# A gated linear recurrence with a maxout feed-forward block: which units run beside which group of matmuls

## The chip, the cores and the metric

The kernel runs on one core of a Trainium2 chip. The metric is the device time of one execution in microseconds. The core has five engines with instruction streams of their own: TensorE (PE: matmuls, and weight loads, shown as PEld), VectorE (DVE), ScalarE (ACT), GpSimd (POOL) and SyncE (SP, which here only issues DMA transfers). They wait for each other by semaphores. Matmul results go to PSUM, which has banks of 512 float32 values per partition.

## The reference

Two blocks in a row. The first is a recurrence over time for every batch b and head h, with a state matrix of 48 x 48:

```
f = sigmoid(f_logit)                                   # q, k, v, f_logit: (4, 8, 768, 48)
state = f[t][:, None] * state + outer(k[t], v[t])
y[t] = q[t] @ state
```

The second takes y as x with 3072 tokens of 8*48 = 384 features:

```
h = max(x @ w1, x @ w2, x @ w3)                        # w1, w2, w3: 384 x 768
out = h @ w_out                                        # w_out: 768 x 384
```

q, k, v and f_logit are float32. The weights arrive as float64, and the kernel rounds them to float32 itself, word by word.

## The kernel before, in words

**Units and groups.** A chunk is 64 time steps. A unit `u` is one chunk of two batches: 128 tokens with all 8 heads. There are NU = 24 units; even and odd ones belong to two pairs of batches, each with its own running state. Four units (GRP) make 512 tokens, a group for the feed-forward part (FFN); there are six groups, 0 to 5.

**The steps of a unit.** `sigmoids(u)` makes the gates on ScalarE; `scan(u)` makes the products of the gates from behind on VectorE (line 287); `after(u)` multiplies k by them (`kh`, line 298), `before(u)` runs a second scan (line 305) and multiplies q (`qh`, line 309). `keys(u)` turns kh around by four TensorE transposes (line 325) and a ScalarE copy (line 327), or `keys_by_blocks` does the same by 16 transposes of 32 x 32 blocks on VectorE (line 340). `pairs(u)` makes key-query products on TensorE (line 350) and masks them on VectorE (`at`, line 353). `values(u)` multiplies them by v (line 364), makes the new part of the state (line 373) and adds it to the old (`st`, line 381, VectorE); `carry(u)` is the state's decay on GpSimd (line 315). `finish(u)` adds the old state's part to y (line 394) and copies y to `heads` (line 400, ScalarE). The tile `y` has two PSUM banks: columns 0 to 255 of each hold outputs, 256 to 447 the new part of the state. `pack` moves heads into `xT`, the FFN's input, by ten DMA transfers (line 416), since 48 features don't line up with 128 partitions.

**Rows and blocks.** For units below BY_ROWS = 8, f, k and q arrive with tokens on partitions, one transfer a tensor and unit (line 171), and TensorE turns them (line 249). For the others two units arrive together, eight transfers a tensor (line 180), in blocks that VectorE turns (line 254), and the products are GpSimd's.

**The FFN as a generator.** `ffn(g, xT)` is a Python generator. One step makes 128 of the 768 hidden features (j) with one of the three matrices (i): three matmuls (line 443) into one PSUM tile `p`, of which there are two, each a bank. For i = 0 ScalarE copies it to `top` (line 448); for i = 1 and 2 VectorE takes the maximum with it (line 450). float32 matmuls run as two passes, so the trace has two records for each. A step of 512 tokens yields twice, a half-step of 256 tokens once. In group 0 the first two j run by halves, so that the work can start when two units are packed: 12 half-steps. Four output steps follow (matmuls line 469, copy line 472, DMA line 476), with two yields each. Every group has 44 yields.

**The order.** `tc.manual_schedule` takes the order written in the program, on each engine and in each queue. `fill(n)` runs n yields of the oldest FFN generator that is pending. So the numbers of yields say how much FFN work lies on TensorE between the steps of the units. Units 0 to 3 are written out; their gaps on TensorE hold some unused matmuls (`busy`). Then a loop over u = 4 to 23 runs unit u, prepares unit u + 1, and calls fill in between.

**Weights.** `load_weights` fetches them in 24 pieces of 384 KB, nine on GpSimd's queue in the written-out part, the rest on SP's from inside group 0. Each piece is rounded in three parts: `round_begin` (two ScalarE passes, lines 218 and 221), `round_middle` (VectorE's maximum, line 230, and its shift and mask, line 231; GpSimd's addition, line 233) and `round_end` (VectorE, line 240, into `w_in` or `w_out`). Group 0's steps call them ahead of the piece that they need.

Of the kernel before, what the change touches and what calls it, by code (L numbers as in the profile page):

```python
# [11 lines left out]
U32 = mybir.dt.uint32  # L12
# [41 lines left out]
def kernel(  # L54
# [32 lines left out]
    def fast():  # L87
        ctx = ExitStack()
        with ctx:
# [58 lines left out]
            BY_ROWS = 8  # L148
# [65 lines left out]
            def round_begin(n):  # L214
                if n in raw:
                    lo, hi = words(n)
                    top = work.tile([128, PIECE], U32, name="top_bits", bufs=4)
                    nc.scalar.activation(top.bitcast(FP32), hi.bitcast(FP32), AF.Abs)

                    rest = work.tile([128, PIECE], U32, name="rest_bits", bufs=3)  # L220
                    nc.scalar.activation(rest, lo, AF.Copy, scale=2.0 ** -29)
                    halfway[n] = (top, rest)

            def round_middle(n):
                if n in raw:
                    top, rest = halfway[n]

                    nc.vector.tensor_scalar(top.bitcast(FP32), top.bitcast(FP32), HI_MIN, None, op0=ALU.max)  # L230
                    nc.vector.tensor_scalar(top, top, 3, 0x3FFFFFF8, op0=ALU.logical_shift_left, op1=ALU.bitwise_and)  # L231

                    nc.gpsimd.tensor_tensor(top, top, rest, op=ALU.add)  # L233

            def round_end(n):
                if n in raw:
                    (top, _), (_, hi) = halfway.pop(n), words(n)
                    dst = pieces[n][0].bitcast(U32)
                    by = lambda t: t.rearrange("p (a c) -> p a c", a=dst.shape[1])
                    nc.vector.scalar_tensor_tensor(dst, by(hi), 0xC0000000, by(top),  # L240
                                                   op0=ALU.bitwise_and, op1=ALU.bitwise_or)
                    raw.pop(n)
# [76 lines left out]
            def keys(u):  # L319

                if u < min(BY_ROWS, NU - 2):
                    kh = ready[u]["kh"]
                    tr_s = ps_tr.tile([UT, HP, 128], FP32, name="tr")
                    for hp in range(HP):
                        nc.tensor.transpose(tr_s[:, hp, :], kh[:, hp].rearrange("p a t -> p (a t)"), ident)  # L325
                    ks = work.tile([UT, H, DP], FP32, name="ks")
                    nc.scalar.copy(ks.rearrange("s h d -> s (h d)"), tr_s.rearrange("s a d -> s (a d)"))
                    ready[u]["ks"] = ks

            def keys_by_blocks(u, n):  # L330

                if BY_ROWS <= u < NU - 2:
                    kh = ready[u]["kh"]
                    if n == 0:
                        ready[u]["ks"] = work.tile([UT, H, DP], FP32, name="ks")
                    ks = ready[u]["ks"].rearrange("s (hp par) d -> s hp par d", par=2)
                    a, t0 = divmod(n * 32, C)
                    for p0 in range(0, 128, 32):
                        par, e0 = divmod(p0, DP)
                        nc.vector.transpose(ks[n * 32:(n + 1) * 32, :, par, e0:e0 + 32], kh[p0:p0 + 32, :, a, t0:t0 + 32])  # L340
# [82 lines left out]

            def ffn(g, xT):
# [3 lines left out]
                steps = [(j, slice(0, TOK)) for j in range(NJ)]  # L428
                if g == 0:
                    steps = [(j, slice(n * HALF, (n + 1) * HALF)) for n in range(2) for j in range(J_HALF)] + steps[J_HALF:]  # L430
                done, n_step = 2, 0
                for j, t in steps:
                    w = t.stop - t.start
                    for i in range(3):
                        p = ps_f.tile([128, TOK], FP32, name="p")[:, 0:w]
                        for kt in range(NK):
                            if g:
                                rhs = xT[:, kt, :]
                            elif w < TOK:
                                rhs = by_halves(xT)[:, t.start // HALF, kt, :]  # L440
                            else:
                                rhs = by_halves(xT)[:, :, kt, :]
                            nc.tensor.matmul(p if g or w < TOK else p.rearrange("p (two t) -> p two t", two=2),  # L443
# [22 lines left out]
                for i in range(GRP):  # L466
                    p = ps_f.tile([128, TOK], FP32, name="p")
                    for j in range(NJ):
                        nc.tensor.matmul(p[:, 0:DM], lhsT=hm[:, j, i * UT:(i + 1) * UT], rhs=w_out[:, j, :],  # L469
                                         start=(j == 0), stop=(j == NJ - 1))  # L470
                    o = work.tile([UT, DM], FP32, name="o", bufs=3)
                    nc.scalar.copy(o, p[:, 0:DM])  # L472
                    c, bp = divmod(g * GRP + i, 2)
                    for a in range(2):
                        t0 = (2 * bp + a) * S + c * C
                        nc.sync.dma_start(out=out[t0:t0 + C, :], in_=o[a * C:(a + 1) * C, :])
                    yield
                    yield
# [24 lines left out]
            with tc.manual_schedule():  # L503
# [26 lines left out]
                load_weights(3, queue=nc.gpsimd)  # L530
# [9 lines left out]
                after(3)  # L540
                pairs(2)
                finish(1)
                carry(3)
                load_weights(3, queue=nc.gpsimd)
# [4 lines left out]
                for n in range(2):  # L549
                    round_begin(n)  # L550
                values(2)
                keys(3)
                finish(2)
                round_middle(0)
                load_weights(1, queue=nc.gpsimd)
                pairs(3)
# [3 lines left out]
                load_weights(1, queue=nc.gpsimd)  # L560
# [20 lines left out]
                fill(2)  # L581
# [3 lines left out]
                for u in range(GRP, NU):  # L585
                    n = u + 1
                    fill(0 if u == 2 * GRP else 4 if u % 2 and u > 2 * GRP else 2)
                    keys(u)
                    keys_by_blocks(u, 2)
                    if u > GRP:  # L590
                        finish(u - 1)
                        if u % GRP == 3:
                            pack(0, 2, xT)
                        elif u % GRP == 0:
                            pack(3, 3, xT, both)
                    if u % GRP == 0:
                        if u > GRP:
                            pending.append(ffn(u // GRP - 1, xT))
                        xT = new_xT()
                    pairs(u)  # L600

                    if u + 2 < BY_ROWS:
                        load(u + 2)
                    if BY_ROWS <= u + 3 < NU and u % 2:
                        load(u + 3, one, "fkq" if u % GRP == 1 else "f")
# [5 lines left out]
                    fill(2)  # L611
# [4 lines left out]
                    fill(2)  # L616
                    if BY_ROWS <= u + 2 < NU and u % GRP == 0:
# [4 lines left out]
                    fill(1 if u < 2 * GRP else 2)  # L622
                    if BY_ROWS <= u + 2 < NU and u % GRP == 0:
                        load(u + 2, one, "q")
                    keys_by_blocks(n, 0)
                    if u >= 2 * GRP:
                        fill(2)
# [236 lines left out]
```

## Time and profile before

Three runs: 480.65, 481.89 and 482.61 us, median 481.89.

| | |
|---|---|
| profiled execution | 480.5 us |
| its span, first to last instruction | 478.8 us |
| TensorE busy | 456.6 us, 95% |
| VectorE busy | 282.8 us, 59% |
| GpSimd, ScalarE busy | 113.1 us, 102.4 us |
| first FFN matmul | at 34.56 us |
| group 0's last output matmul ends | at 123.6 us |
| last matmul ends, end of the span | 472.1 us, 478.8 us |
| all FFN matmuls (lines 443 and 469) | 290.0 us and 96.3 us busy |
| TensorE clock granted, mean | 0.992 of full speed |

The span is the time from the first instruction to the last; the metric adds 1.7 us in this execution. Busy time sums an engine's instructions. A row of a timeline gives start, duration, engine, line, operation, output and inputs, and in brackets how long the engine had been idle before it and what released it. TensorE's ends are modelled, so two neighbouring rows can overlap a little.

### The profile page before, as it was taken

The page shows a single profiled execution, that of the slowest core. Times are in us where ns is not written, and L with a number is a line of the kernel's source. Part 1 is how long each engine was busy: PE and PEld are TensorE (multiplying, and loading weights), DVE is VectorE, ACT ScalarE, POOL GpSimd, SP SyncE. Part 2 cuts the span into 40 slices and gives each one's busy share as a digit, 9 for nine tenths or more (in the row PEclk, how much of TensorE's full clock was granted, in tenths as well). Part 3 has the DMA queues.
Part 4 walks back from the last instruction along what each step waited for, and adds up shares of the span by engine and source line. Part 5 has one row for each costly group of instructions (what it writes and reads, how often), then busy time and mean ns, then how long its engine had stood idle before and what let it go on. Part 6 is the DMA issues. An engine that isn't in the chain of part 4 may idle for free.

```text
span 478.8 us, 10137 instructions
## 1 busy us (share of the span) xinstructions
PE 456.6 (95%) x4061; PEld 248.5 (52%) x4061; DVE 282.8 (59%) x565; ACT 102.4 (21%) x217; POOL 113.1 (24%) x133
## 2 busy tenths in 40 slices
PE   5978799899999999999999999999999999999994
PEld 4766655556445446555445555445554445444452
DVE  6949998977487584487684587684585210112100
ACT  2546345422012102012102112112112102000000
POOL 2546553441330230330230330330331200000000
PEclk9989999999999999999999999999999999999998
DMA  9997997614466043673042674042620012100012
GB/s 135 211 212 219 200 329 113 89 40 65 99 95 94 12 79 78 104 89 50 2 79 56 112 89 68 1 78 56 117 34 2 1 49 51 33 1 0 1 28 45
DMA packets 167578, 38.53 MB, mean 80 GB/s; under 512 B 154752, under 2 KB 165888, under 8 KB 167520
## 3 DMA queue, kind: packets, MB, share of 16 engines
q1 hardware_dynamic: 162032, 33.16, 39.9%
q0 software_dynamic: 1008, 3.54, 2.7%
q10 hardware_dynamic: 4480, 1.08, 1.5%
q8 instruction: 34, 0.56, 0.5%
q14 instruction: 24, 0.20, 0.1%
HBM read 28.31 MB, written 4.72 MB: 69 GB/s over the span
## 4 chain that ended last, share of the span: by engine, by line
PE 83%; SPq 8%; DMA 4%; DVE 2%; issue 1%; ACT 1%; POOL 0%; DVEq 0%; ACTq 0%; POOLq 0%
PE p L443 52%; PE p L469 20%; PE y L364 3%; PE y L394 2%; SPq L171 2%; SPq L180 2%; PE y L373 2%; PE a L350 2%; DMA q_ld<-in_q_dram 2%; SPq L161 2%; DMA v_ld<-in_v_dram 2%; SPq L416 1%; PE tr L249 1%; PE tr L325 0%; DMA k_ld<-in_k_dram 0%
## 5 line engine op out<-in xcount | busy, mean ns | idle before, releaser
L443 PE MATMUL p<-xT,w_in 128*128 128x512 f32 (+1 forms) x684 | 290.0, 575 | 2.9 <-DVE w_in L240 1.6
L443 PEld LDWEIGHTS p<-xT,w_in 128*128 128x128 f32 x684 | 126.3, 190 | 137.2 <-issue 125.2
L469 PE MATMUL p<-w_out,hm 128*128 128x384 f32 x288 | 96.3, 489 | 0.0
L450 DVE TENSOR_TENSOR top<-p,top 128x512 f32<-128x512 f32 (+1 forms) x38 | 25.0, 657 | 99.5 <-PE p L443 99.5
L469 PEld LDWEIGHTS p<-w_out,hm 128*128 128x128 f32 x288 | 54.0, 190 | 37.6 <-issue 1.9
L340 DVE STREAM_TRANSPOSE ks<-kh 32x128 f32<-32x128 f32 x224 | 67.7, 302 | 3.6
L448 ACT COPY top<-p 128x512 f32<-128x512 f32 (+1 forms) x38 | 21.4, 563 | 175.6 <-PE p L443 175.6
L297 POOL COPY ends<-r 128x8 f32<-128x8 f32 x24 | 7.5, 310 | 186.8 <-DVE r L287 186.8
L450 DVE TENSOR_TENSOR hm<-p,top 128x512 f32<-128x512 f32 (+1 forms) x38 | 24.8, 652 | 29.5 <-PE p L443 29.4
L298 POOL TENSOR_TENSOR kh<-kt,r 128x512 f32<-128x512 f32 x16 | 31.4, 1962 | 36.5 <-DVE kt L254 26.1
L400 ACT COPY heads<-y 64x256 f32<-64x256 f32 (+1 forms) x72 | 26.6, 369 | 48.1 <-PE y L394 34.5
L233 POOL TENSOR_TENSOR top_bits<-top_bits,rest_bits 128x384 uint32<-128x384 uint32 x24 | 28.1, 1171 | 35.6 <-DVE top_bits L231 33.3
L287 DVE TENSOR_TENSOR_SCAN r<-gate,from_one 128x520 f32<-128x520 f32 x24 | 30.6, 1276 | 5.3 <-issue 2.5
L472 ACT COPY o<-p 128x384 f32<-128x384 f32 x24 | 11.4, 476 | 102.4 <-PE p L469 98.7
L305 DVE TENSOR_TENSOR_SCAN prod<-gate,from_inv 128x520 f32<-128x520 f32 x24 | 30.1, 1256 | 0.0
L364 PEld LDWEIGHTS y<-at,v_ld 64*64 64x64 f32 x768 | 13.6, 134 | 18.3 <-issue 15.4
L353 DVE TENSOR_TENSOR at<-a,mask 128x512 f32<-128x512 f32 x24 | 16.6, 691 | 8.3 <-PE a L350 7.9
L254 DVE STREAM_TRANSPOSE gate<-sig 128x512 f32<-128x512 f32 x16 | 11.3, 705 | 15.3 <-ACT sig L269 15.3
L394 PEld LDWEIGHTS y<-qh,state 48*48 48x48 f32 x704 | 11.8, 123 | 15.2 <-issue 13.3
L364 PE MATMUL y<-at,v_ld 64*64 64x64 f32 x768 | 17.1, 225 | 2.7 <-DMA v_ld<-in_v_dram 2.7
L315 POOL TENSOR_TENSOR state<-st,ends 128x384 f32<-128x384 f32 x22 | 19.4, 881 | 0.1
L309 POOL TENSOR_TENSOR qh<-qt,prod 128x512 f32<-128x512 f32 x16 | 18.8, 1176 | 0.8 <-DVE qt L254 0.8
(68 smaller groups left out, 271.1 us busy)
## 6 DMA issues: line engine op xcount, KB each, us to landing
v_ld<-in_v_dram SPq DMA_DIRECT2D x48, 96.0 KB, 3.1
out_dram<-o SPq DMA_DIRECT2D x48, 96.0 KB, 2.3
raw<-in_moe_w_dram POOLq DMA_DIRECT2D x9, 384.0 KB, 6.3
raw<-in_moe_w_dram SPq DMA_DIRECT2D x9, 384.0 KB, 4.7
raw<-in_moe_w_out_dram SPq DMA_DIRECT2D x6, 384.0 KB, 8.0
xT<-heads SPq DMA_DIRECT2D x30, 72.0 KB, 2.1
f_ld<-in_f_logit_dram SPq DMA_DIRECT2D x32, 64.0 KB, 2.7
k_ld<-in_k_dram SPq DMA_DIRECT2D x32, 64.0 KB, 2.6
```

The source lines that it names most:

```text
L233: nc.gpsimd.tensor_tensor(top, top, rest, op=ALU.add)
L287: nc.vector.tensor_tensor_scan(r[:, 0:LEN][:, ::-1], flat(gate)[:, ::-1], flat(from_one)[:, ::-1], 1.0, op0=ALU.mult, op1=ALU.max)
L298: (nc.vector if u < BY_ROWS else nc.gpsimd).tensor_tensor(kh.rearrange("p h a t -> p a h t"), kt, by_batch(r[:, 1:LEN + 1].rearrange("p (x ...
L305: nc.vector.tensor_tensor_scan(flat(prod), flat(gate_tiles[u % 2]), flat(from_inv[u % 2]), 1.0, op0=ALU.mult, op1=ALU.max)
L340: nc.vector.transpose(ks[n * 32:(n + 1) * 32, :, par, e0:e0 + 32], kh[p0:p0 + 32, :, a, t0:t0 + 32])
L364: nc.tensor.matmul(y[o:o + DP, a, hp * C:(hp + 1) * C], lhsT=v_ld[s, 2 * hp + par, :], rhs=d["at"][s, par, hp, :], start=(hp == 0), stop=F ...
L394: nc.tensor.matmul(y[o:o + D, a, hp * C:(hp + 1) * C], lhsT=st[r, a, hp, :], rhs=d["qh"][r, a, hp, :], start=False, stop=(hp == HP - 1), s ...
L400: nc.scalar.copy(heads[o, :, t0 + a * C:t0 + (a + 1) * C], y[i, a, 0:HP * C].rearrange("p (h t) -> p h t", h=HP))
L443: nc.tensor.matmul(p if g or w < TOK else p.rearrange("p (two t) -> p two t", two=2), lhsT=w_in[i][:, kt, j * 128:(j + 1) * 128], rhs=rhs, ...
L448: nc.scalar.copy(top, p)
L450: nc.vector.tensor_tensor(hm[:, j, t] if i == 2 else top, p, top, op=ALU.max)
L469: nc.tensor.matmul(p[:, 0:DM], lhsT=hm[:, j, i * UT:(i + 1) * UT], rhs=w_out[:, j, :], start=(j == 0), stop=(j == NJ - 1))
```

## The change

It has six parts.

1. BY_ROWS is 6, not 8: units 6 and 7 arrive in blocks. A new number BY_BLOCKS = 12 says where `keys_by_blocks` takes over from `keys`: units 6 to 11 have their inputs in blocks but their keys turned by TensorE.
2. Fills: more yields of group 0 go ahead of and into unit 4; two to each gap in units 5 to 11, one to the last gap of units 10 and 11. From unit 12 on the amounts are those of before.
3. Group 1 runs by halves throughout: 18 half-steps and two output steps for units 4 and 5, then the same for units 6 and 7. It is appended in unit 6, after a pack of units 4 and 5; units 6 and 7 are packed in unit 8. It comes to lie beside units 7 to 12.
4. Two half-steps in a row share one PSUM tile, one bank: columns 0 to 255, then 256 to 511. This holds in group 0 too.
5. Weights: the first six pieces are issued together after the gates of unit 3; the next ones and the first roundings move behind the pairs of unit 3.
6. The maximum of `round_middle` reads one tile (`size`) and writes another (`top_bits`), which is 3 x 128 with gaps, where it worked in place on 384 elements in a row. The later operations see it as 3 x 128.

```diff
-            BY_ROWS = 8
+            BY_ROWS = 6
+            BY_BLOCKS = 12
...
-                    top = work.tile([128, PIECE], U32, name="top_bits", bufs=4)
-                    nc.scalar.activation(top.bitcast(FP32), hi.bitcast(FP32), AF.Abs)
+                    size = work.tile([128, PIECE], FP32, name="size", bufs=2)
+                    nc.scalar.activation(size, hi.bitcast(FP32), AF.Abs)
...
+                    top = work.tile([128, 3, PIECE // 3 + 2], U32, name="top_bits", bufs=2)[:, :, 0:PIECE // 3]
-                    nc.vector.tensor_scalar(top.bitcast(FP32), top.bitcast(FP32), HI_MIN, None, op0=ALU.max)
+                    nc.vector.tensor_scalar(top.bitcast(FP32), size, HI_MIN, None, op0=ALU.max)
                     nc.vector.tensor_scalar(top, top, 3, 0x3FFFFFF8, op0=ALU.logical_shift_left, op1=ALU.bitwise_and)
-                    nc.gpsimd.tensor_tensor(top, top, rest, op=ALU.add)
+                    nc.gpsimd.tensor_tensor(top, top, rest.rearrange("p (a c) -> p a c", a=3), op=ALU.add)
...
-                if u < min(BY_ROWS, NU - 2):
+                if u < min(BY_BLOCKS, NU - 2):
...
-                if BY_ROWS <= u < NU - 2:
+                if BY_BLOCKS <= u < NU - 2:
...
+                whole, half = slice(0, TOK), [slice(n * HALF, (n + 1) * HALF) for n in range(2)]
+                steps = [(j, whole) for j in range(NJ)] + [(i, None) for i in range(GRP)]
                 if g == 0:
-                    steps = [(j, slice(n * HALF, (n + 1) * HALF)) for n in range(2) for j in range(J_HALF)] + steps[J_HALF:]
+                    steps = [(j, half[n]) for n in range(2) for j in range(J_HALF)] + steps[J_HALF:]
+                elif g == 1:
+                    steps = [s for n in range(2) for s in [(j, half[n]) for j in range(NJ)] + [(2 * n + i, None) for i in range(2)]]
...
-                        p = ps_f.tile([128, TOK], FP32, name="p")[:, 0:w]
+                        if w == TOK or n_half % 2 == 0:
+                            bank = ps_f.tile([128, TOK], FP32, name="p")
+                        p = bank[:, n_half % 2 * w:][:, 0:w]
+                        n_half += w < TOK
...
-                load_weights(3, queue=nc.gpsimd)
...
                 after(3)
+                load_weights(6, queue=nc.gpsimd)
...
-                load_weights(3, queue=nc.gpsimd)
...
-                for n in range(2):
-                    round_begin(n)
                 values(2)
                 keys(3)
                 finish(2)
+                pairs(3)
+                round_begin(0)
+                round_begin(1)
                 round_middle(0)
-                load_weights(1, queue=nc.gpsimd)
-                pairs(3)
                 busy(2)
                 round_begin(2)
                 round_middle(1)
-                load_weights(1, queue=nc.gpsimd)
+                load_weights(2, queue=nc.gpsimd)
...
-                fill(2)
+                fill(3)
                 before(GRP)
...
-                    fill(0 if u == 2 * GRP else 4 if u % 2 and u > 2 * GRP else 2)
+                    fills = (2, 2, 2, 1 if 3 * GRP - 2 <= u < 3 * GRP else 2)
+                    if u == GRP:
+                        fills = (3, 3, 3, 3)
+                    elif u >= 3 * GRP:
+                        fills = (4 if u % 2 else 2, 2, 2, 2, 2)
+                    fill(fills[0])
...
-                        if u % GRP == 3:
+                        if u == GRP + 2:
+                            pack(0, 1, xT, one, 0)
+                            pending.append(ffn(1, xT))
+                        elif u == 2 * GRP:
+                            pack(2, 3, xT, one, 1)
+                        elif u % GRP == 3 and u > 2 * GRP:
                             pack(0, 2, xT)
                         elif u % GRP == 0:
                             pack(3, 3, xT, both)
+                            pending.append(ffn(u // GRP - 1, xT))
...
-                    if u + 2 < BY_ROWS:
+                    if u < BY_ROWS - 2:
                         load(u + 2)
-                    if BY_ROWS <= u + 3 < NU and u % 2:
-                        load(u + 3, one, "fkq" if u % GRP == 1 else "f")
+                    elif u == BY_ROWS - 2:
+                        load(u + 2, one, "f")
+                    if u + 3 < NU and u % 2:
+                        load(u + 3, one, "fkq" if u % GRP == 1 and u > 2 * GRP else "f")
```

## The prediction

> **What bounds the kernel now.** I read the page first: span, busy shares, and the slices of TensorE.
>
> ```profile
> span 478.8 us, 10137 instructions
> PE 456.6 (95%) x4061; PEld 248.5 (52%) x4061; DVE 282.8 (59%) x565; ACT 102.4 (21%) x217; POOL 113.1 (24%) x133
> PE   5978799899999999999999999999999999999994
> ```
>
> TensorE is the bound. From the tenth slice on (about 110 us) every slice is a 9, so later work is worth only what TensorE itself does. The idle time lies earlier. The timeline of TensorE gives its places (start, duration, instruction; in brackets the idle time before it and what ended it):
>
> ```profile
> 24.80 0.33 PE L364 MATMUL y<-at,v_ld 64*64 64x64 f32 x4 [1.04 <-DMA v_ld<-in_v_dram]
> 26.77 0.67 PE L364 MATMUL y<-at,v_ld 64*64 64x64 f32 x26 [1.64 <-DMA v_ld<-in_v_dram]
> ...
> 45.93 2.76 PE L443 MATMUL p<-xT,w_in 128*128 128x256 f32 x12
> 49.96 0.63 PE L249 MATMUL tr<-ident,q_ld 128*128 128x128 f32 x4 [1.27 <-DMA q_ld<-in_q_dram]
> ...
> 54.46 2.86 PE L443 MATMUL p<-xT,w_in 128*128 128x256 f32 x12 [1.19 <-DVE hm L450]
> ```
>
> By windows, TensorE idles 5.6 us in 0:12, then 9.9 us in all from 12 to 144, and about 6.7 us after its last matmul. Between 36 and 96 the VectorE is busy 55 of 60 us: it rounds weights and serves units 4 to 8. Every change can win at most those 9.9 us, some cold-clock time at 27 to 32, and TensorE work removed.
>
> Two more lines decide this case. Both touch the PSUM tile y: line 381 reads columns 256 to 447, line 394 writes columns 0 to 255, and line 394 reads nothing that 381 makes.
>
> ```profile
> 84.63 0.55 DVE L381 TENSOR_TENSOR st<-y,state 128x384 f32<-128x384 f32 x1
> ...
> 85.33 0.66 PE L394 MATMUL y<-qh,state 48*48 48x64 f32 x32 [1.51 <-DVE st L381]
> ```
>
> TensorE waits nevertheless, and starts 0.15 us after the read ends (0.14 and 0.15 at the two other places, 33.97 and 109.52). So the program's waits go by bank, not by column.
>
> **The Trainium skill** says this on the operations concerned. "PSUM — Partial Sum Buffer", section "PSUM bank collisions raise a hardware error", says that two engines may not touch one bank in the same quadrant at once even at different columns, and that reads and writes have to be guarded by bank. The three waits agree. "VectorE: DVE Perf Modes", section "What auto-detection actually checks": the double-rate mode of a one-source operation needs outermost sizes of source and destination that are both even or equal. "SBUF — State Buffer", section "Who interferes with whom": in that mode VectorE excludes GpSimd. The trace agrees: line 230 takes 0.35 us alone and 0.83 to 1.16 us when GpSimd's line 233 runs, mean 608 ns. "TensorE: Matmul & The Clock Gate", Part 1: an idle array is clocked down to half; here four transposes took 1.11 us at 28.31 against 0.66 before.
>
> **The change, part by part.** Against the profiled execution: 478.8 us of span, 1.7 us around it, 480.5 in all, 1.4 below the median of 481.9.
>
> *Weights later.* GpSimd issued three pieces (1.2 MB) at 16.67, beside the loads of v. Moved behind the gates of unit 3, all six go out from 21.4 on, 0.78 us each. The loads of v for units 2 and 3 then meet no weights: the 1.04 and 1.64 us and about 1.5 us of slow clock go. But piece 0 lands near 27 instead of 23, GpSimd's state product of unit 3, queued behind the six issues, moves to 26 (needed at 30), and the ten transfers into xT share the DMA engines with all six pieces (they took 22.60 to 31.99). I put the first FFN matmul at 33.5 instead of 34.56: **-1.1 us**. Bounds: -2.5 (xT by 32), +2 (pieces starve it). The first roundings also move behind the pairs of unit 3: ScalarE copies keys 3 and heads 2 first, VectorE masks unit 3 first; both pull unit 3 forward and are in the 33.5.
>
> *Gapped maximum.* Destination 3 by 128 against source 384: no double rate, so about 0.55 us (line 240's duration for 384 elements), but no wait for GpSimd. Where pieces follow each other, the cycle falls from 1.94 us (starts 37.97, 39.91) to about 1.75, set by GpSimd's 1.18 us plus issue.
>
> *Two half-steps in one PSUM bank.* Before, each half-step of group 0 had its own bank of two. Now an odd one writes the bank from which the even one before it is being read, and by the waits above it must stand until that read is done: 0.16 us from last matmul to the read (47.27 to 47.43), 0.37 (ScalarE) or 0.42 us (VectorE) of reading, 0.14 us back. That is 0.7 us, if the reader is free, and more if it is queued. In group 0's first six half-steps three such waits replace the waits on weights (0.45, 0.32, 0.37, 0.47): even. In the next six I find 0.75, 0.25 and 2.5 us (the last read stands behind unit 4's scan and products on VectorE), against 1.27 and 1.19 us that go. With the 1.1 us above, keys of unit 4 start again near 57.2: the early gain is spent, **+1.1**.
>
> *Rest of group 0 with three units.* Of its idle time after 57 us (1.51, 0.80 and 0.1 to 0.2 beside) about half goes, since VectorE has less to do: **-1.2** (0 to -2.4). Its block loads are eight issues per tensor (4.2 to 6.2 us of SP), for units 6 and 7 some 15 us of SP; they are needed from about 78 us on and start near 63: hidden; if late, 1 to 2 us. Group 1's xT now comes in two packs of ten transfers on SP (6.3 us each, as at 101.38), in units 6 and 8; the first is used a unit later, the second two units later: hidden, else 2 us each. Fewer buffers for the rounding (two, not four) hold, since VectorE reuses them in its own order: 0, at worst a ScalarE pass of 0.56 us that waits.
>
> *Rows and blocks.* Units 6 and 7 lose twelve transposes each on TensorE (0.49, 0.44 and 0.44 us per tensor: 1.37 us a unit), units 8 to 11 gain four for the keys (0.53 us): -2.7 + 2.1 = **-0.6**. VectorE loses 64 transposes of 302 ns and ScalarE gains four copies; TensorE hides that. Units 6 and 7 put 1.96 and 1.18 us each on GpSimd, more than ten us ahead of need.
>
> *Group 1 by halves.* 216 passes of 256 columns at 0.2242 us (12 from 54.46 to 57.15) against 108 of 512 at 0.4458 (132.45 to 137.80): **+0.3**. Then its 36 half-steps h0 to h35. By the amounts of fill, h0 falls into unit 7; each unit runs two half-steps, keys, finish and pairs, then four, values, and two more. TensorE has no other work inside the four or between the last two and the next first two. So in each unit (a) the third of the four waits for the second's read, (b) one wait lies across the unit's border, and (c) sometimes one is left behind values. VectorE's queue behind the pairs decides (a):
>
> ```profile
> 101.07 0.69 DVE L353 TENSOR_TENSOR at<-a,mask 128x512 f32<-128x512 f32 x1 [0.62 <-PE a L350]
> ...
> 101.77 0.63 ACT L269 ACTIVATE sig<-f_ld 128x512 f32<-128x512 f32 x1
> 102.43 0.71 DVE L254 STREAM_TRANSPOSE gate<-sig 128x512 f32<-128x512 f32 x1 [0.67 <-ACT sig L269]
> 103.18 1.24 DVE L287 TENSOR_TENSOR_SCAN r<-gate,from_one 128x520 f32<-128x520 f32 x1
> 104.45 0.21 DVE L290 RECIPROCAL from_inv<-r 128x8 f32<-128x8 f32 x1
> 104.58 0.65 DVE L450 TENSOR_TENSOR hm<-p,top 128x512 f32<-128x512 f32 x1
> ```
>
> A maximum behind a scan starts 3.65 us after the pairs (104.58 less 100.93). Two half-steps take 2.7 us, so a third that waits for two maxima starts near 4.5 instead of 2.7. Full steps, with 2.7 us in the other bank, never felt this. Walking it through: h3 0.7, h7 0.7 (ScalarE reads), h9 0.4, h11 0.7, h15 1.95, h17 0.7, h19 0.7, h21 1.35, h23 0.7, h25 0.7, h27 2.3 (behind transposes and second scan of unit 12), h29 0.7, h33 1.45, h35 0.35. Sum **+12.7 us**. Bounds: 7 (ten waits of 0.7), 17 (each read queued).
>
> Sum: -1.1 + 1.1 - 1.2 - 0.6 + 0.3 + 12.7 = +11.2: 491.7 from the profiled execution, 493.1 from the median. I take 492.5.
>
> **Rivals.** *The bare wait* (0.2): reads are seldom queued, ten waits of 0.7 us, so 7.0 instead of 12.7: +5.5, 487. *Weights too late* (0.11): pieces 0 to 5 land in a row (384 KB at 220 GB/s, 1.8 us each, from 27 on) behind xT, the first half-steps run at that pace, +3 to +4 on top: 496. For it: the DMA share is 0.92 to 1.33 until 36 us. *Columns, not banks* (0.10): an odd half-step doesn't wait. Then group 1 costs 0.3, group 0's half-steps win 2.5 (1.19 and 1.27), and -1.1 - 2.5 - 1.2 - 0.6 + 0.3 = -5.1: 477. It decides as soon as group 1's 18 odd half-steps wait less than 2.5 us together, 0.14 each; line 394's waits speak against it. *Even* (0.07): waits of about 3 us in all and the gains cancel, 481.
>
> **How the numbers follow.** The main case has 0.52 and spans 488 to 496. The range must reach the bare wait and late weights, with the bounds of queueing: 482 to 499; outside lies mostly the faster case. A difference of 0.5% (2.4 us) is about what a measurement of this kernel can tell from none. Faster 0.10, same 0.07, slower 0.83.
>
> **What would show it.** Right: from about 112 to 185 us TensorE, before without gaps, shows idle times of 0.6 to 2.5 us ahead of 256-column matmuls of line 443, released by the copy or the maximum of the same bank, every second one; no waits on v near 25 us; line 230 near 550 ns throughout. Wrong: half-steps back to back in group 1, or idle time released by weights or xT.

## The result, and the profile after

The changed kernel takes 502.3 us (median of 500.74, 501.22, 503.37 and 504.75) against 482.25 us of the kernel before, measured beside it. The ratio is 1.042 with an interval of 1.036 to 1.048: 20 us slower. The forecast was 492.5 us, with a range to 499. The direction held, the size did not: it was 11 us, and it is 20.

The page of the changed kernel: span, busy times, TensorE's slices, and the TensorE clock granted in the same 40 slices.

```profile
span 502.8 us, 10373 instructions
PE 465.6 (93%) x4161; PEld 270.8 (54%) x4161; DVE 267.4 (53%) x515; ACT 106.6 (21%) x227; POOL 115.5 (23%) x137
PE   5968699999989878799999999999999999999994
PEclk9989899999999999799999999999999999999999
```

The profiled execution took 504.75 us, the longest of the four, so its span is 24.0 us above that of before. Two things have changed on TensorE. It is no longer full: of the slices from the twelfth to the seventeenth, all 9 before, only one still is. And it is busy 9.0 us longer, though the change's own additions to its work come to -0.3 us by the prediction's count: some passes (a float32 matmul is two in the trace) ran slower. The clock row says where: a 7 in the seventeenth slice, and one more 8 among the first five. The windows of TensorE give the same account in three stretches (columns: length, busy time and records, clock granted, DMA share, GB/s), first before, then after:

```profile
0.00:60.00 60.00, 46.91 (x654) 0.97 1.05 196
60.00:120.00 60.00, 57.69 (x727) 1.00 0.62 127
120.00:216.00 96.00, 95.89 (x849) 1.00 0.52 81
```

```profile
0.00:60.00 60.00, 43.68 (x606) 0.94 1.00 200
60.00:120.00 60.00, 59.32 (x565) 0.97 0.54 110
120.00:216.00 96.00, 82.61 (x977) 0.95 0.44 70
```

Idle time grows by 3.2 us up to 60 us, falls by 1.6 us from 60 to 120, and grows by 13.3 us from 120 to 216, where group 1 runs by halves. What it waited for, by the view of TensorE's waits (sum, number, longest):

```profile
PE p L473 <- DVE hm L480: 12.1, 7, 5.0
...
PE p L473 <- DVE top L480: 5.3, 5, 2.9
PE p L473 <- ACT top L478: 3.0, 6, 0.7
PE p L473 <- DMA xT<-heads: 1.5, 1, 1.5
PE y L400 <- DVE st L387: 1.3, 2, 1.2
PE y L379 <- issue: 1.0, 1, 1.0
```

Line 473 is the FFN matmul (443 before), 480 the maximum (450), 478 ScalarE's copy (448), 422 the transfers of `pack` (416), 275 the sigmoid (269). The three rows of the matmul with `hm` and `top` are 20.4 us of waits for the reader of a PSUM bank, where the kernel before had one of 1.2 us. The waits on v are gone. Group 1 in the timeline:

```profile
127.58 2.86 PE L473 MATMUL p<-xT,w_in 128*128 128x256 f32 x12 [0.52 <-DVE hm L480]
135.19 2.86 PE L473 MATMUL p<-xT,w_in 128*128 128x256 f32 x12 [0.46 <-ACT top L478]
...
151.44 2.86 PE L473 MATMUL p<-xT,w_in 128*128 128x256 f32 x12 [1.73 <-DVE hm L480]
...
186.31 2.69 PE L473 MATMUL p<-xT,w_in 128*128 128x256 f32 x6 [2.04 <-DVE hm L480]
```

This is the forecast picture: waits ahead of 256-column matmuls, released by the copy or the maximum. They are ahead of half-steps 3, 7, 15 and 27 of group 1, counted from 0 as in the prediction. The last row has something that was not forecast: six passes took 2.69 us, where six take 1.56 elsewhere. And one place is of another kind:

```profile
196.75 0.69 DVE L359 TENSOR_TENSOR at<-a,mask 128x512 f32<-128x512 f32 x1
197.31 3.21 ACTq L422 DMA_DIRECT2D xT<-heads  x5
...
200.57 0.63 ACT L275 ACTIVATE sig<-f_ld 128x512 f32<-128x512 f32 x1 [3.29 <-DMA xT<-heads]
...
203.85 0.42 DVE L480 TENSOR_TENSOR hm<-p,top 128x256 f32<-128x256 f32 x1
...
204.33 5.49 PE L473 MATMUL p<-xT,w_in 128*128 128x256 f32 x12 [5.00 <-DVE hm L480]
```

Unit 12's turn packs unit 11 with five transfers on ScalarE's queue. ScalarE issues them for 3.2 us, and the sigmoid of unit 13 stands behind; VectorE's scan waits for the sigmoid, the maximum for the scan (both in VectorE's order), and TensorE for the maximum, 5.00 us, ahead of half-step 33. Then 12 passes take 5.49 us instead of 2.86. The same hold-up of ScalarE was there before, and cost nothing, because 8 us of output matmuls covered it:

```profile
182.99 8.01 PE L469 MATMUL p<-w_out,hm 128*128 128x384 f32 x24
...
183.83 3.33 ACTq L416 DMA_DIRECT2D xT<-heads  x5
187.21 0.63 ACT L269 ACTIVATE sig<-f_ld 128x512 f32<-128x512 f32 x1 [3.40 <-DMA xT<-heads]
```

### The profile page after: what moved, and what is told of

It reads as the page before. It is cut to its first block, busy times and chain, and to the rows that moved or that the text cites. A ratio compares the mean times of both kernels' runs of the same rounds, so it can differ in the third digit from the quotient of the medians.

```text
span 502.8 us, 10373 instructions
## 1 busy us (share of the span) xinstructions
PE 465.6 (93%) x4161; PEld 270.8 (54%) x4161; DVE 267.4 (53%) x515; ACT 106.6 (21%) x227; POOL 115.5 (23%) x137
## 4 chain that ended last, share of the span: by engine, by line
PE 82%; DVE 5%; SPq 4%; DMA 3%; ACT 2%; issue 2%; ACTq 1%; DVEq 0%
PE p L473 54%; PE p L433 19%; PE y L370 3%; PE y L400 2%; DMA xT<-heads 2%; PE y L379 2%; PE a L356 2%; SPq L162 1%; DVE r L293 1%; SPq L172 1%; DMA f_ld<-in_f_logit_dram 1%; DVE prod L311 1%; SPq L422 1%; PE tr L331 1%; ACT heads L406 1%
## 5 line engine op out<-in xcount | busy, mean ns | idle before, releaser
L473 PE MATMUL p<-xT,w_in 128*128 128x512 f32 (+1 forms) x792 | 301.9, 533 | 21.9 <-DVE hm L480 12.1
L473 PEld LDWEIGHTS p<-xT,w_in 128*128 128x128 f32 x792 | 150.3, 196 | 147.4 <-issue 105.8
L346 DVE STREAM_TRANSPOSE ks<-kh 32x128 f32<-32x128 f32 x160 | 48.3, 302 | 2.6
L304 POOL TENSOR_TENSOR kh<-kt,r 128x512 f32<-128x512 f32 x18 | 34.4, 1913 | 34.8 <-DVE kt L260 31.5
L237 POOL TENSOR_TENSOR top_bits<-top_bits,rest_bits 128x384 uint32<-128x384 uint32 x24 | 26.2, 1092 | 36.6 <-DVE top_bits L235 26.9
L260 DVE STREAM_TRANSPOSE gate<-sig 128x512 f32<-128x512 f32 x18 | 12.8, 710 | 17.6 <-ACT sig L275 17.6
L315 POOL TENSOR_TENSOR qh<-qt,prod 128x512 f32<-128x512 f32 x18 | 21.2, 1180 | 0.2 <-DVE qt L260 0.2
```

What stands on the lines that cost most here:

```text
L237: nc.gpsimd.tensor_tensor(top, top, rest.rearrange("p (a c) -> p a c", a=3), op=ALU.add)
L304: (nc.vector if u < BY_ROWS else nc.gpsimd).tensor_tensor(kh.rearrange("p h a t -> p a h t"), kt, by_batch(r[:, 1:LEN + 1].rearrange("p (x ...
L473: nc.tensor.matmul(p if g > 1 or w < TOK else p.rearrange("p (two t) -> p two t", two=2), lhsT=w_in[i][:, kt, j * 128:(j + 1) * 128], rhs=rhs,
```

## The experiments

Twelve kernels were timed in four groups, each beside the kernel before on the same chip. Ratios are to that, with their 95% intervals. The kernel before had medians of 482.25 to 483.48 us in these groups, so rows of different groups are better compared by their ratios.

| kernel | median us | ratio | interval |
|---|---|---|---|
| the change | 502.3 | 1.042 | 1.036 to 1.048 |
| change, unit 11's pack on SP | 496.1 | 1.026 | 1.023 to 1.030 |
| and own banks in group 1 | 491.6 | 1.016 | 1.011 to 1.022 |
| and own banks in group 0 | 488.0 | 1.011 | 1.007 to 1.015 |
| and weights as before | 487.8 | 1.011 | 1.008 to 1.014 |
| change, own banks only | 494.5 | 1.024 | 1.021 to 1.027 |
| change, unused matmuls in two waits | 499.4 | 1.034 | 1.031 to 1.038 |
| before, shared banks in group 0 | 485.5 | 1.006 | 1.003 to 1.009 |
| before, weights later | 482.4 | 0.999 | 0.998 to 1.001 |
| before, gapped maximum | 484.6 | 1.002 | 1.000 to 1.004 |
| before, rows and blocks | 487.0 | 1.008 | 1.005 to 1.011 |
| the same, all packs of the loop on SP | 487.8 | 1.009 | 1.005 to 1.012 |
| rows and blocks, fills moved forward | 483.1 | 1.001 | 1.000 to 1.003 |

**A bank of its own for each half-step**, in both groups. This was the prediction's main cause, undone.

```diff
-                        if w == TOK or n_half % 2 == 0:
-                            bank = ps_f.tile([128, TOK], FP32, name="p")
-                        p = bank[:, n_half % 2 * w:][:, 0:w]
-                        n_half += w < TOK
+                        p = ps_f.tile([128, TOK], FP32, name="p")[:, 0:w]
```

> The changed kernel with one part undone: every half-step takes a PSUM bank of its own, of the two, as group 0's did before. Theory (waits by bank, and the cold clock that follows them): the waits of every second half-step go; idle time of TensorE in group 1 falls from 13.4 us to under 4, the slow clock there goes (about 5 us), group 0's half-steps win 4 to 6 us; 480 to 485. Rival (half-steps are too short for VectorE's queue, whichever bank): most waits stay, 494 to 500. Rival (later weights make the loss): early part unchanged, 488 to 492.

494.5 us: 8 us of the 20 are gone, and more than half remain. The theory that the shared bank is the whole loss fell here; the time lies in the range of the first rival. TensorE's idle time from 120 to 216 us falls from 13.4 to 8.2 us, not to under 4. In group 1 the short waits vanish, four stay:

```profile
133.01 2.86 PE L470 MATMUL p<-xT,w_in 128*128 128x256 f32 x12 [1.21 <-DVE hm L477]
147.81 2.86 PE L470 MATMUL p<-xT,w_in 128*128 128x256 f32 x12 [1.20 <-DVE top L477]
168.78 4.15 PE L470 MATMUL p<-xT,w_in 128*128 128x256 f32 x18 [1.15 <-DVE top L477]
193.76 5.49 PE L470 MATMUL p<-xT,w_in 128*128 128x256 f32 x12 [4.48 <-DVE top L477]
```

The last is the place of ScalarE's transfers, slow passes included. The other three are VectorE's queue behind the pairs: `ps_f`, the pool of the tiles `p`, has two banks, so with banks of their own a half-step has only the 1.35 us of the one between as cover.

**The shared bank alone, in the kernel before** (there only group 0 has half-steps).

```diff
...
-                        p = ps_f.tile([128, TOK], FP32, name="p")[:, 0:w]
+                        if w == TOK or n_half % 2 == 0:
+                            bank = ps_f.tile([128, TOK], FP32, name="p")
+                        p = bank[:, n_half % 2 * w:][:, 0:w]
+                        n_half += w < TOK
```

> The kernel before with this alone: group 0's twelve half-steps share a bank in pairs. Theory: waits of 0.5 to 3 us behind each first half, the keys of unit 4 start 4 to 6 us later than at 57.2, part of it by slow clock; 486 to 489. Rival (columns count, the early loss is from the weights): no change, 482.

485.5 us, a little under the expectation: +2.7 us. Its waits are 1.02 and 0.46 us for ScalarE's copy and 0.71, 0.76, 2.92 and 0.59 us for the maximum. The long one is a read queued on VectorE, the kind for which the prediction had 2.5 us in these half-steps, and the passes behind it are slow (4.54 us for twelve, 2.86 at full speed).

**The pack in unit 12's turn on SP alone.**

```diff
-                            pack(3, 3, xT, both)
+                            pack(3, 3, xT, one if u == 3 * GRP else both)
```

> The changed kernel, but the last pack into group 2's xT (unit 12) is issued on SP alone and not on ScalarE's queue too. Theory: the longest wait of group 1 (5.0 us at 204.3) is ScalarE's sigmoid standing behind five DMA issues (3.3 us); without them it falls to about 1.7 us and the slow clock behind it shrinks; -4 to -6 us against the changed kernel, 496 to 498. Rival (VectorE's own queue sets that wait): within 1 us.

496.1 us: 6.2 us less than the change (1.6% by the ratios, 7.5 us), as expected of ScalarE's transfers. The wait is 1.74 us and the passes behind it are at full speed:

```profile
186.04 1.56 PE L473 MATMUL p<-xT,w_in 128*128 128x256 f32 x6 [2.04 <-DVE hm L480]
...
195.06 6.28 SPq L422 DMA_DIRECT2D xT<-heads  x10
195.44 0.63 ACT L275 ACTIVATE sig<-f_ld 128x512 f32<-128x512 f32 x1
...
199.21 2.86 PE L473 MATMUL p<-xT,w_in 128*128 128x256 f32 x12 [1.74 <-DVE hm L480]
```

The first row is half-step 27. Its wait is 2.04 us as in the change, but here the passes behind it take 1.56 us, not 2.69.

**Unused matmuls in the two long waits of group 1**: four ahead of its half-step 27 and nine ahead of 33. Nothing is left out.

```diff
+                        idle = {28: 4, 34: 9}.get(n_half, 0) if g == 1 else 0
+                        if idle:
+                            spare = ps_tr.tile([128, TOK], FP32, name="tr")
+                            for _ in range(idle):
+                                nc.tensor.matmul(spare[:, 0:256], lhsT=ident, ...)
```

> The changed kernel with unused matmuls put into the two longest waits of group 1: four of 256 columns (1.8 us) ahead of half-step h27, nine (4.0 us) ahead of h33. The waits' length stays. Theory (the clock falls in a long wait and costs as much again after it): the matmuls behind them run at full speed, 4 to 5 us less than the changed kernel, 497 to 498. Rival (the modelled ends only show it): no gain, 502 to 503.

499.4 us. The matmuls still wait for the same maximum, but then run at full speed:

```profile
184.39 1.89 PE L470 MATMUL tr<-from_one,ident 128*128 128x256 f32 x8
186.60 1.56 PE L479 MATMUL p<-xT,w_in 128*128 128x256 f32 x6 [0.32 <-DVE hm L486]
...
197.86 4.05 PE L470 MATMUL tr<-from_one,ident 128*128 128x256 f32 x18
203.02 2.86 PE L479 MATMUL p<-xT,w_in 128*128 128x256 f32 x12 [1.11 <-DVE hm L486]
```

So about 3 us of the loss are slow passes behind these two waits, somewhat less than expected. (By the records of the changed kernel they were 1.13 and 2.63 us.) The two ratios' intervals overlap a little, 1.036 to 1.048 and 1.031 to 1.038, so the rows above carry this reading more than the times do.

**Own banks, and the pack on SP**: the first and third edits together.

> The changed kernel with a bank for every half-step and the pack of unit 12 on SP alone. Theory (the 4.5 us wait that is left in group 1 with own banks is ScalarE's sigmoid behind DMA issues, plus slow clock): it falls to about 1.2 us like the other three; 6 us less than with own banks alone, 487 to 489. Rival (VectorE's queue behind unit 12's transposes): 1 us less, 493.

488.0 us. The two gains add up: 502.3 - 494.5 = 7.8 and 502.3 - 496.1 = 6.2 make 14.0, and 14.3 were measured. Group 1's waits are now 1.22, 1.20, 1.15 and 1.45 us, 5.0 us together. The rows show the first and the last, and ahead of the first VectorE's mask behind the pairs and the maximum that ends the wait:

```profile
128.09 0.69 DVE L359 TENSOR_TENSOR at<-a,mask 128x512 f32<-128x512 f32 x1 [1.04 <-PE a L356]
...
131.59 0.38 DVE L477 TENSOR_TENSOR hm<-p,top 128x256 f32<-128x256 f32 x1
...
132.03 2.86 PE L470 MATMUL p<-xT,w_in 128*128 128x256 f32 x12 [1.22 <-DVE hm L477]
...
189.76 2.86 PE L470 MATMUL p<-xT,w_in 128*128 128x256 f32 x12 [1.45 <-DVE top L477]
```

That is about as much as this kernel still loses to the one before (1.1%, 5.2 us). So the traces say that half-steps are dear even without sharing. No kernel with whole steps in group 1 and the rest of the change was run, so this share is read from the waits and not isolated. Up to 120 us the trace has 0.3 us more idle time than that of before, and over the whole span TensorE is busy 1.3 us longer.

**And the written-out part of before** for weights and first roundings, on top of that.

```diff
-                load_weights(6, queue=nc.gpsimd)
+                load_weights(3, queue=nc.gpsimd)
...
+                load_weights(3, queue=nc.gpsimd)
...
```

> As the run before it, with the weights' issues and the first roundings where the kernel before had them. If the later weights are a loss (a stop of TensorE for instructions at line 379 of 1.0 to 2.5 us, xT late, slow clock after it): 2 to 3 us less, 484 to 486. If they are a gain, as the prediction had it (waits on v of 1.04 and 1.64 us return): 1 to 2 us more, 489 to 490.

487.8 us, no difference; neither expectation came true. The two waits at the values of unit 2 are back (1.9 us for v, and 1.1 us that the profile puts down to ScalarE where the kernel before has 1.04 us for v), and TensorE's stop in the middle of line 379 is gone.

**Weights and first roundings later, alone, on the kernel before.**

> The kernel before with the later weights and first roundings alone. Prediction's step: the first FFN matmul 1 us earlier, 481 to 482. Rival (six pieces together hold up TensorE's instructions and xT): the stop at the products of values(3) appears, the first FFN steps wait and run at the slow clock; 483 to 486.

482.4 us: 0.5 us less by the ratio, with an interval from 1.2 us less to 0.2 us more. The waits on v are gone and the first FFN matmul is early, but the old state is waited for 1.57 us at 32.34, line 373 stops for 0.72 us, and passes are slow up to 39 us. Keys of unit 4 start at 56.97 against 57.15.

**The gapped maximum alone.**

> The kernel before with the gapped maximum alone. Prediction's step: the cycle from piece to piece falls from 1.94 to 1.75 us, the waits on rounded weights at the first half-steps (0.45, 0.32, 0.37, 0.47) shrink by half, the maximum takes 0.55 us throughout; 480.5 to 482. Rival (no effect on TensorE's path): 482.8.

484.6 us: no gain, and the interval leaves room for a loss of up to 0.4%. The maximum takes 543 ns (608 before) and GpSimd's addition 1102 (1171), the mask 467 (411). The waits on `w_in` fall from 1.6 to 0.7 us in all. Values of unit 2 stand 1.3 us behind line 218, ScalarE's write of `size`. That is hardly a new wait: the kernel before stands 1.04 us for v at the same matmul, and the next kernel below, with the maximum in place and four buffers, 0.85 us behind the same write of ScalarE.

**Rows and blocks alone, on the kernel before.**

```diff
-            BY_ROWS = 8
+            BY_ROWS = 6
+            BY_BLOCKS = 12
...
+                    elif u == BY_ROWS - 2:
+                        load(u + 2, one, "f")
...
-                    if BY_ROWS <= u + 2 < NU and u % GRP == 0:
+                    if u + 2 < NU and (u % GRP == 0 or u == GRP + 2):
```

> The kernel before with units 6 and 7 loaded by blocks (rows up to unit 6, keys transposed on TensorE up to unit 12) and nothing else of the change. The prediction's step: 2.7 us of gate waits gone, 2.1 us more of matmuls, 0.6 us less, so ratio 0.999. Rival: the loads by blocks move to SP's queue between the first group's weights and delay those, or the keys of units 8 to 11 on TensorE cost more than the waits gave: 484 to 486. If TensorE's idle time between 60 and 120 us falls from 2.3 us to about 0.7 as in the changed kernel, this part is what made it fall there.

487.0 us: slower than the rival's range too. Idle time did not fall between 60 and 120 us; it rose between 72 and 96, from 1.5 to 5.4 us:

```profile
81.17 1.18 POOL L234 TENSOR_TENSOR top_bits<-top_bits,rest_bits 128x384 uint32<-128x384 uint32 x1 [0.76 <-DVE top_bits L232]
...
82.29 1.14 POOL L298 COPY ends<-r 128x8 f32<-128x8 f32 x1
83.40 1.19 POOL L299 TENSOR_TENSOR kh<-kt,r 128x512 f32<-128x512 f32 x1
84.64 0.66 PE L326 MATMUL tr<-ident,kh 128*128 128x128 f32 x4 [2.05 <-POOL kh L299]
85.05 0.71 DVE L255 STREAM_TRANSPOSE qt<-q_ld 128x512 f32<-128x512 f32 x1 [1.60 <-DMA f_ld<-in_f_logit_dram]
...
88.01 0.55 DVE L382 TENSOR_TENSOR st<-y,state 128x384 f32<-128x384 f32 x1
88.62 1.11 PE L395 MATMUL y<-qh,state 48*48 48x64 f32 x32 [3.32 <-DVE st L382]
```

GpSimd makes the products of unit 6 now. In its queue they stand behind an addition of the rounding, which itself waited for VectorE, and they come late for unit 6's keys. The old state comes later still, by 3.32 us, and part of that has another cause: VectorE, which adds to the state (line 382) in its own order, had stood 1.60 us ahead of turning q. The profile names a transfer of f; the blocks of q were issued just before it on SP, from 78.59 to 82.79 us, and took 2.2 to 2.7 us to land. So late loads have a share in it (the rival had them delay the weights). Slow passes follow (1.11 instead of 0.66 us).

**The same with fills moved forward**, since the change has more group 0 work ahead of unit 6.

```diff
-                fill(2)
+                fill(3)
                 before(GRP)
...
-                    fill(0 if u == 2 * GRP else 4 if u % 2 and u > 2 * GRP else 2)
+                    fills = {4: (3, 2, 2, 2), 5: (2, 2, 2, 2), 6: (2, 1, 1, 1), 7: (2, 1, 1, 1)}.get(u, (2, 2, 2, 2))
+                    fill(0 if u == 2 * GRP else 4 if u % 2 and u > 2 * GRP else fills[0])
...
```

> The rows-and-blocks kernel (487.0, ratio 1.008) with the fill amounts moved forward as in the change: one more yield of group 0 ahead of unit 4's second scan, 3, 2, 2, 2 in unit 4, 2, 2, 2, 2 in unit 5, and fewer in units 6 and 7 (2, 1, 1, 1), so that six yields remain for unit 8 as before; group 1 by whole steps. If the 4 us that rows and blocks cost alone are only the gap at 82 to 89 us, where GpSimd's product of unit 6 comes 2.05 us late and the old state 3.32 us late, then more FFN work ahead of it covers them: near 483, ratio 1.000, with the gap gone. Rival: the products on GpSimd come late whatever the fill, or the work is missing in units 6 and 7: 485 to 488.

483.1 us: the 4 us are covered again, and nothing is gained. The gap at 82 to 89 us is down to 0.51 us; but GpSimd's keys are late by 0.84 and 1.47 us at 101 and 110 us, where the moved work is missing, as the rival had it, without the rival's time.

**Rows and blocks, with units 8, 12, 16 and 20 packing on SP alone.**

```diff
-                            pack(3, 3, xT, both)
+                            pack(3, 3, xT, one)
```

> The kernel before with the rows and blocks of the change, and the pack of units 8 and 12 on SP alone, so that no DMA issue of the xT stands ahead of ScalarE's sigmoid there. In the kernel before that wait of 3.3 us is covered by whole steps: no gain beyond the rows alone, the same time as those within 0.5%. Rival: ScalarE's queue was the last cover used up, and 1 to 3 us are gained: 479 to 481.

487.8 us, the same as rows and blocks alone. With whole steps on that place, ScalarE's transfers cost nothing that this can tell (the two intervals are 1.005 to 1.012 and 1.005 to 1.011). The 6 us belong to the half-steps that lie there after the change.

**Own banks in group 1 alone**, with the pack on SP; group 0 still shares.

```diff
+                        if w == TOK or g == 1:
+                            n_half = 0
                         if w == TOK or n_half % 2 == 0:
...
-                            pack(3, 3, xT, both)
+                            pack(3, 3, xT, one if u == 3 * GRP else both)
```

> The changed kernel with a bank of its own for every half-step of group 1 alone (group 0's twelve half-steps still share), and the pack of unit 12's turn on SP alone. It stands between 496.1 (both groups share) and 488.0 (neither does). The prediction put all the cost of sharing into group 1 and 0 us on the start of unit 4's keys: by it this kernel is near 488. The reading of the traces puts 5 us into group 1 (10.3 us of TensorE's waits between 120 and 216 us against 5.2) and about 3 us into group 0: 491, with a wait near 2.9 us ahead of the first whole step of group 0.

491.6 us, the reading of the traces. Two rows of its timeline show both halves of it:

```profile
59.40 5.83 PE L475 MATMUL p<-xT,w_in 128*128 128x256 f32 x12 [2.94 <-DVE top L482]
...
134.67 2.86 PE L475 MATMUL p<-xT,w_in 128*128 128x256 f32 x12 [1.22 <-DVE hm L482]
```

Group 0 has its long wait and slow passes as in the change. From there on the kernel is that with own banks everywhere, 2.6 us later (134.67 against 132.03).

So the 20 us divide like this, by the ratios of the first four rows of the table: 7.5 us ScalarE's transfers ahead of a half-step (6.2 by the medians), 4.9 us sharing in group 1 (4.5), 2.7 us sharing in group 0 (3.6), and 5.2 us that stay. Each row's interval is 3 to 6 us wide, so the third share is not clear of nothing by itself; the shared bank alone cost the kernel before as much, 2.7 us (0.3 to 0.9%). That the 5.2 us are half-steps with two banks is read from the waits (5.0 us). Each share contains its own slow passes. No version beat the kernel before.

## Why the prediction was right in direction and wrong in size

In the two profiled executions the span grew by 24.0 us, where the sum had 11.2. Of the 12.8 us between, 9.3 are slow passes, which the sum put at nothing, and 3.2 are idle time up to 60 us, where it had gain and loss cancel. Group 1's waits are 0.6 us above the sum, the idle time from 60 to 120 us is 0.4 below it. By medians the difference is smaller, 20 against 11, since the profiled execution of the changed kernel was its longest.

**The bank rule: right. Group 1's sum: near, by luck.** TensorE waits for the reader of its bank although it writes other columns, as the prediction read it from the waits of line 394; with a bank for each half-step the short waits were gone. (Each pair of half-steps is one tile in one bank; no run tells apart which of the two the wait goes by.) Group 1's waits were put at 12.7 us and came to 13.4. The fourteen terms as listed add up to 13.4, not 12.7, and that they meet the measured sum is two errors that cancel: half-step 33 was put far too low, the other thirteen at 11.95 us, and they came to 8.4. The rows: a bare wait costs 0.46 to 0.59 us, not 0.7; half-steps 9, 17 and 35 did not wait; 15 and 27 were near (1.95 and 2.3 forecast, 1.73 and 2.04 measured).

**Half-step 33: mis-sized, 1.45 forecast and 5.00 measured.** The profile before showed what was missing: ScalarE standing 3.40 us behind its own transfers. It was left out because it had cost nothing, and the change put 256-column steps where 8 us of output matmuls had covered it. Without the transfers it was 1.74 us, near the forecast. With the slow passes behind it this place is worth 6.2 us by the medians, 7.5 by the ratios, the most of any one place.

**The slow clock: a term that the sum did not have.** The prediction named the half clock of an idle array for the start of the kernel and then priced every later wait at its length. In the profiled execution slow passes cost about 9 us (busy time up by 9.0, work down by 0.3). This is the largest step that failed. Some 4 us lie in group 0's start, 1.1 and 2.6 in the matmuls right behind the waits of half-steps 27 and 33.

**Group 0's start: +1.1 and -1.1 forecast, so nothing; the keys of unit 4 come about 6 us late.**

```profile
29.57 0.56 PE L379 MATMUL y<-v_ld,ks 64*64 64x48 f32 x23 [1.00 <-issue]
...
34.30 2.16 PE L473 MATMUL p<-xT,w_in 128*128 128x256 f32 x4 [1.46 <-DMA xT<-heads]
36.93 4.26 PE L473 MATMUL p<-xT,w_in 128*128 128x256 f32 x12 [0.46 <-ACT top L478]
...
59.89 5.83 PE L473 MATMUL p<-xT,w_in 128*128 128x256 f32 x12 [2.94 <-DVE top L480]
65.56 0.60 PE L331 MATMUL tr<-ident,kh 128*128 128x128 f32 x4
```

The FFN starts at 32.14, 1.4 us earlier than forecast. But keys of unit 4, forecast near 57.2, start at 65.56, and at 62.9 without the whole step (2.65 us) that the fills put ahead of them. The bank waits of the twelve half-steps are 6.3 us where 5.1 were forecast; the transfer into xT adds 1.46, slow passes the rest (2.16 us for four, 4.26 us for twelve, 5.83 us for what takes 4.0). Sharing is about half of it: with own banks and the pack on SP these keys start at 62.42. Not all of such a delay stays in the total, where sharing in group 0 cost 2.7 us.

**Weights later: -1.1 forecast, -0.5 measured alone** (0.999, 0.998 to 1.001), which tells neither nothing nor the forecast from it. On top of own banks and the pack it made no difference. The waits on v went as forecast; by the traces what is late next (the old state, the stop in line 379, slow passes) took most of it back: unit 4's keys start 0.2 us earlier.

**Rows and blocks, and the rest of group 0: -0.6 and -1.2 forecast.** The second shows in the changed kernel (idle time from 60 to 120 us down by 1.6). The first was wrong by itself: 4 us slower, and level once the fills follow. The step "more than ten us ahead of need" failed there: behind the additions of the rounding, GpSimd's products came 2.05 us late for unit 6, and of the loads that were to be hidden, q's kept VectorE 1.60 us. In the changed kernel itself neither wait is left.

**Gapped maximum: 0.55 us forecast, 0.54 measured**, and, as forecast, no gain in time that the run could tell.

**The rivals.** Columns, not banks (477): excluded by the waits. Its price was also wrong in its own terms. With a bank of its own for each half-step, and ScalarE's transfers out of the way, the time is 488.0, not 477. That group 1 by halves costs only 0.3 us when nothing is shared is a step that failed: its waits alone are 5.0 us then. Late weights (496) came nearest in number, but not for its reason: no wait on a weight is left in the changed kernel's list.

## What to carry to other kernels

When large steps are cut into small ones, look at the trace for every wait of the other engines that a large step covers now, also those that cost nothing, and ask which of them the small step will uncover. Price a wait of TensorE with the slow passes that can follow it, not with its length alone: here 2.04 us of waiting cost 1.1 us more in one trace and nothing more in another, and 5.00 us cost 2.6 us more. And what frees a small step's bank counts for as much as the bank: two of them with 1.35 us of work each could not cover a queue of about 3.6 us on VectorE.

## What the runs showed of the hardware that was not expected

**Slow passes came after less idle time than expected, and not every time.** The Trainium skill ("TensorE: Matmul & The Clock Gate", Part 1) gives an idle window of about 3.4 us for the step down to half rate. In the changed kernel a wait of 2.04 us, with TensorE busy on both sides, was followed by six passes in 2.69 us instead of 1.56. With TensorE kept busy in that wait the passes took 1.56 us. But with the pack on SP the same wait, 2.04 us long, was followed by six passes in 1.56 us. Two kernels with own banks show such a pair too: six passes of 512 columns took 4.54 us behind a wait of 2.18 us (weights later), and 2.84 us behind one of 2.17 us (weights as before). So the length of a wait near 2 us did not decide it, and what did is not shown here.

**TensorE stopped in the middle of a run of matmuls that waited for nothing.** In all seven kernels whose weights are issued together, line 379 (373 in the kernel before) stops after its ninth matmul for 0.6 to 2.5 us, and the trace names no releaser ("issue", 1.00 us in the row above). It does not in those with the weights as before. In each of the seven, a queue that the profile calls "instruction" has one transfer that starts 2.3 to 2.8 us ahead of the stop's end, while the weight pieces fill the DMA engines (in the change their mean busy share is 0.95 and 1.01 from 24 to 28 and from 28 to 32 us). The Trainium skill ("Runtime: NRT & Kernel Launch", "Instruction fetch mechanics") says that instructions come in blocks by a DMA queue of the sequencer's own, mostly hidden. A fetch that is late behind the weights fits this, but no run tested it.
